# A planned attention and feed-forward kernel: another order of work, other assumptions about loads, and one third of a batch transposed by DMA

## The chip, the cores and the metric

The kernel runs on one core of one Trainium2 chip. The metric is device time in microseconds (us) of one execution. Engines: TensorE (PE for its matmuls, PEld for its weight loads), VectorE (DVE), ScalarE (ACT), GpSimd (POOL) and SyncE (SP). In this kernel POOL issues the loads and SP the stores and the DMA transposes; ScalarE issues two stores at the very end. Each engine executes its instructions in the order in which the program lists them.

## What is computed

An attention with squared relu, and a gated feed-forward block on its result:

```python
scores = np.matmul(q, k.transpose(0, 1, 3, 2)) / np.sqrt(64)
attn_out = np.matmul(np.maximum(scores, 0.0) ** 2 / 448, v)     # q, k, v: (8, 12, 448, 64) float32
x = attn_out.transpose(0, 2, 1, 3).reshape(8 * 448, 768)
out = (gelu(x @ w_gate) * (x @ w_val)) @ w_out                   # 768 x 1536 twice, 1536 x 768
```

The output is 3584 x 768 in float32.

## The kernel before

The inputs are loaded by casting DMAs to bf16. A batch of 448 tokens and 12 heads is handled in thirds of four heads, written (b, m). For a third, q and k are loaded (two DMAs), transposed to qkT, multiplied to scores (`add_scores`, L692), passed through relu on ScalarE (L729) and squared on VectorE (L738), and multiplied with v (`add_values`, L768), which gives x transposed. All products use 64 x 64 quarters of the array and go through the helper on L397. Work called lo uses one row half of the array and work called hi the other, and the two halves run beside each other.

A third is transposed in one of two ways. `add_transposes` (L644) does it on TensorE, in two groups of 14 transposes (L662), with a copy on VectorE after each (L666). `add_dma_transposes` (L490) regroups q and k with one copy on VectorE (L499), and SP then issues two DMA transposes (L504). Batches 0 and 1 go through TensorE, later ones by DMA, except for the thirds listed in `ON_PE` (L350). A DMA transpose waits until the load issued last before it has landed, and a load waits for the DMA transposes issued before it ("pace").

The feed-forward part of batches 0 and 1 is computed plainly (`add_gate_value`, L1002), that of the batches from 2 on partly in pairs with seven products instead of eight (`add_pair`, L893), with sums of weights (ws) and of x (ts) made on VectorE. The second matrix (`add_product`, L1149) is done in 14 groups gr of 256 tokens, in seven products named 1 to 7 (chain 1 7 2 6 4 5 3), also from sums (wt, s). Each product's bank is read into osb, by a copy on ScalarE or VectorE (L1217) or an addition on VectorE (L1215). When both halves of a row tile are done, SP stores it with two DMAs, one for each half of 64 rows (L1233). The first tile of the last group is stored by column halves, one part by SP and one by ScalarE.

The weights w_gate and w_val come in six chunks (`load_w12`, L433: wg, then wv), called w0 to w5 here, and w_out in four (`load_wo`, L442). The order of all loads after those of batch 0 is written out in `LOADS` (L30): w is the next chunk of both weights, q the next third's q and k, v the next third's v, o the next chunk of w_out. POOL issues them in that order. qk16 has room for two thirds: a load of q and k has to wait until the transposes of the third two before it have read theirs. v has room for three. At most eight loads are in flight.

The order of TensorE's units after the start is planned before anything runs. `LINE` (L12) is a list of units in order of preference. `run_plan` (L104) plays the whole program through with a cost for each operation, takes among the first 60 units of the list the one that can start earliest, and puts ScalarE's, VectorE's and SP's operations in the order in which they become ready. What it assumes of loads: the bytes over a rate (`arrivals`), one after the other, 2.0 us to landing, and a margin (`LATE`, 1.0) for loads after batch 0. The order found in this way is fixed in the program; the plan's times are not.

## Time and profile before

| | |
|---|---|
| median of 3 runs | 405.67 us (404.91 to 411.33) |
| the profiled execution | 406.31 us |
| its span, first to last instruction | 404.5 us |
| granted clock of TensorE, mean | 0.998 |
| products on L397, from the first to the last | 6.5 to 399.2 us |
| transposes of q and k on TensorE (L662) | 15 groups, 7.4 to 63.8 us |
| DMA transposes | 32, 74.6 to 291.3 us |

How to read the rows below. In the slices each digit is the busy share of a fortieth of the span, in tenths. A row of waits gives the engine, the operation and line that waited, what it waited for, then us in total, times, and the longest. A row of a stretch gives its bounds, its length, and for each engine the busy time with the number of instructions in brackets (with a line as filter, PE and PEld of that line alone), then granted clock, DMA share and GB/s. A row of the chain of waits gives start, duration and what ran. A row of the timeline gives start, duration, engine, line and operation, out<-in, and in square brackets the idle time before it and what ended it. A row of groups gives busy time, the mean in ns, and the idle time before with its releasers. PEq, SPq and ACTq are sequencers, which issue DMAs.

### The profile page before, as it was taken

What the parts mean: (1) busy time and instruction counts of PE and PEld (TensorE: products, weight loads), DVE (VectorE), ACT (ScalarE), POOL (GpSimd) and SP (SyncE); (2) the same over time, 40 slices, a digit from 0 to 9 for tenths busy, and PEclk for the clock granted to TensorE, in tenths of its full rate; (3) what the DMA queues carried; (4) which work ended last, traced back from release to release, by engine and by line L of the source; (5) the groups of instructions that cost most, each with busy time, mean ns of one, the idle gap of its engine ahead of it and who ended that gap; (6) DMA issues with size and microseconds to landing.
All of it is one profiled execution on the core that took longest, in us unless ns stands there. A gap on an engine that the chain in (4) does not pass through costs nothing.

```text
span 404.5 us, 18664 instructions
## 1 busy us (share of the span) xinstructions
PE 394.6 (98%) x8533; PEld 347.7 (86%) x8536; DVE 299.4 (74%) x514; ACT 244.9 (61%) x367; POOL 74.0 (18%) x120
## 2 busy tenths in 40 slices
PE   7999999999999999999999999999999999999994
PEld 3456887998999978889999899999999999889993
DVE  2886885977778858889867698787977865777562
ACT  4856684675676676657876667584776643553120
POOL 7547432140122201310312103110110000000000
PEclk9999999999999999999999999999999999999999
DMA  7999999597569787824777988744551321000245
GB/s 104 156 176 196 198 196 138 103 174 127 96 90 181 132 149 119 121 53 73 95 142 95 235 137 137 109 64 71 45 98 42 81 55 29 2 3 3 62 120 138
DMA packets 71567, 43.94 MB, mean 109 GB/s; under 512 B 32448, under 2 KB 68032, under 8 KB 71488
## 3 DMA queue, kind: packets, MB, share of 16 engines
q0 software_dynamic: 37152, 24.39, 44.3%
q1 hardware_dynamic: 34176, 18.16, 22.0%
q8 instruction: 67, 1.10, 1.1%
q10 hardware_dynamic: 160, 0.20, 0.1%
q14 instruction: 12, 0.10, 0.1%
HBM read 48.76 MB, written 11.01 MB: 148 GB/s over the span
## 4 chain that ended last, share of the span: by engine, by line
PE 88%; DMA 7%; DVE 1%; issue 1%; POOL 1%; ACT 0%; SPq 0%; DVEq 0%; POOLq 0%
PE ff L397 77%; PE sp L397 7%; DMA qk<-in_k_dram 4%; DMA wv<-in_moe_w_val_dram 2%; PE sp L662 1%; PE ff L1395 1%; DMA qkT<-qkr 1%; PE ff L583 1%; POOL qk L457 1%; PE ff L662 0%; DVE qkr L499 0%; DVE osb L1217 0%; DVE uT L1028 0%; DVE attnT L738 0%; PE ff L625 0%
## 5 line engine op out<-in xcount | busy, mean ns | idle before, releaser
L397 PE MATMUL ff<-xT,wg 64*64 64x448 bf16 x1872 | 189.2, 350 | 0.5 <-DVE uT L1028 0.5
L729 ACT ACTIVATE attnT<-sp 128x896 bf16<-128x896 f32 x168 | 152.0, 919 | 48.5 <-PE sp L397 47.3
L397 PE MATMUL ff<-xT,wv 64*64 64x448 bf16 x1440 | 153.5, 350 | 0.5 <-DMA wv<-in_moe_w_val_dram 0.4
L397 PEld LDWEIGHTS <-wv 64*64 64x64 bf16 x1872 | 111.3, 107 | 11.7 <-DMA wv<-in_moe_w_val_dram 0.8
L397 PEld LDWEIGHTS <-wg 64*64 64x64 bf16 x1872 | 110.6, 107 | 10.4 <-issue 0.8
L738 DVE TENSOR_TENSOR attnT<-attnT 128x1792 bf16<-128x1792 bf16 (+1 forms) x98 | 92.3, 953 | 15.5 <-ACT attnT L729 15.1
L397 PE MATMUL ff<-attnT,v 64*64 64x448 bf16 (+1 forms) x768 | 83.8, 327 | 0.1
L397 PEld LDWEIGHTS <-s 64*64 64x64 bf16 x1344 | 80.9, 107 | 2.0
L397 PE MATMUL sp<-qkT 64*64 64x448 bf16 (+1 forms) x768 | 77.2, 333 | 0.8 <-ACT qkT L633 0.6
L397 PE MATMUL ff<-wo,s 64*64 64x384 bf16 x672 | 61.6, 323 | 0.0
L397 PEld LDWEIGHTS <-uT 64*64 64x64 bf16 x912 | 54.4, 107 | 1.4 <-issue 0.7
L397 PE MATMUL ff<-wt,s 64*64 64x384 bf16 x672 | 53.9, 323 | 0.0
L397 PE MATMUL ff<-ts,ws 64*64 64x448 bf16 x432 | 52.8, 349 | 0.0
L397 PE MATMUL ff<-ts,wv 64*64 64x448 bf16 x432 | 51.8, 349 | 0.4 <-DVE ts L876 0.4
L472 POOL DMA_DIRECT2D v<-in_v_dram x48 | 29.7, 628 | 119.3 <-ACT attnT L729 54.7
L397 PEld LDWEIGHTS <-v 64*64 64x64 bf16 x768 | 46.9, 107 | 4.1 <-issue 0.4
L397 PE MATMUL ff<-wo,uT 64*64 64x384 bf16 x576 | 48.1, 323 | 0.4 <-issue 0.4
L1028 DVE TENSOR_TENSOR uT<-gel,ff 128x448 bf16<-128x448 bf16 x60 | 37.0, 618 | 14.1 <-PE ff L397 12.4
L1023 ACT ACTIVATE gel<-ff 128x448 bf16<-128x448 f32 x60 | 32.5, 542 | 21.2 <-PE ff L397 20.0
L397 PEld LDWEIGHTS <-qkT 64*64 64x64 bf16 x768 | 37.9, 107 | 7.3 <-issue 3.9
L397 PEld LDWEIGHTS <-ws 64*64 64x64 bf16 x648 | 40.6, 106 | 3.4
L945 DVE TENSOR_TENSOR part<-ff,part 128x448 f32<-128x448 f32 x54 | 32.8, 621 | 9.3 <-PE ff L397 6.6
(60 smaller groups left out, 382.4 us busy)
## 6 DMA issues: line engine op xcount, KB each, us to landing
out_dram<-osb SPq DMA_DIRECT2D x54, 192.0 KB, 3.2
v<-in_v_dram POOLq DMA_DIRECT2D x48, 128.0 KB, 5.3
qk<-in_q_dram POOLq DMA_DIRECT2D x23, 224.0 KB, 5.2
qk<-in_k_dram POOLq DMA_DIRECT2D x23, 224.0 KB, 5.7
wg<-in_moe_w_gate_dram POOLq DMA_DIRECT2D x6, 384.0 KB, 9.4
wv<-in_moe_w_val_dram POOLq DMA_DIRECT2D x6, 384.0 KB, 10.1
wo<-in_moe_w_out_dram POOLq DMA_DIRECT2D x4, 576.0 KB, 9.5
qkT<-qkr SPq DMA_TRANSPOSE x32, 3.3
```

Source lines behind the costliest of these rows:

```text
L397: return nc.tensor.matmul(o, lhsT, rhs, start=start, stop=stop, skip_group_check=onto, tile_position=(P * row, P * col))
L457: op = load(4 * (h1 - h0) * S * D, lambda: nc.gpsimd.dma_start(tile_of(), src[b, h0:h1].rearrange("h (p c) d -> p h (c d)", c=SC)), deps, ...
L472: return nc.gpsimd.dma_start(v16[b, m][HALF[i], :, :, :], v[b, h0:h1].rearrange("h (p c) d -> p h c d", c=SC)[:, :, c0:c0 + VC, :])
L583: nc.tensor.matmul(t[:, :], warm[:, 0:128], warm[:, :], start=True, stop=True)
L662: nc.tensor.transpose(t[HALF[j], c, :], src[:, 2 * r + j, c, :], ident[:, :], tile_position=(0, P * j))
L729: relu.ins = nc.scalar.activation(duo["a"][:, u % 2, :, :], box[0][:, :, 0:S], AF.Relu).ins
L738: nc.vector.tensor_tensor(a[:, part], a[:, part], a[:, part], op=ALU.mult)
L945: rd.ins = nc.vector.tensor_tensor(t[:, :], box[0][:, 0:S], t[:, :], op=ALU.add).ins
L1023: nc.scalar.activation(gel[b, fc][:, :], box[0][:, 0:S], AF.Gelu)
L1028: u_op[b, fc].ins = nc.vector.tensor_tensor(uT[b][:, fc, :], gel.pop((b, fc))[:, :], box[0][:, 0:S], op=ALU.mult).ins
L1395: nc.tensor.matmul(t[HALF[j], :], warm[:, HALF[j]], warm[:, :], start=True, stop=True, tile_position=(0, P * j))
```

## The change

- The constants that the plan assumes change: a load counts as ready 0.3 us later, a wait for a free slot or for a transpose costs 0.5 us more (`WAKE`), arrivals after batch 0 take 6% longer (`SLOW`), and the margin is 3.0 us instead of 1.0 (`LATER_BY`) except for w0 to w4 and q and v up to third (2,0). The plan now also counts stores as DMA time (`stored`).
- `LOADS` has another order: w0, q and k of (1,0) and (1,1), w1, q and k of (1,2) and (2,0), v of (1,0) and (1,1), w2, w3, w4, v of (1,2) and (2,0), w5, and so on. Before it was q and k of (1,0), w0, q and k of (1,1), v of (1,0), w1, q and k of (1,2), w2, w3, q and k of (2,0), v of (1,1) and (1,2), w4, q and k of (2,1), w5.
- `LINE` has another order of units.
- w_out is loaded in eight DMAs, one for each chunk and column half; products on a half wait for that half.
- `ON_PE` keeps (2,0) alone: (2,1) is transposed by DMA.
- The last read of the last group is split between ScalarE and VectorE, and in the last two groups the second half of each store is issued by ScalarE.

```diff
--- before.py
+++ after.py
@@ -10,25 +10,25 @@
 
 
 LINE = """
-2 o s c2 2D1 s 0 s 0 2E6 o 4F1 0 0 0 s o d5 s 1 1 a1 1 s 5 0 1 b1 o a6 1 0 s a7 f6 0 2D2 1 2C2 0 s
...
+s 1 d4 s 1 s 2C1 s 1 0 2F5 0 0 6A4 s 1 4C2 2D3 2B1 h6 c7 o 1 o 0 0 2F2 a5 o 3 s s s s c6 o a3 2 0
...
 """

 LOADS = """
-q w q v w q w w q v v w q w v v q o o v o q o q v q q v q v q v v q v q v v q q v q v q v q v q v
+w q q w q q v v w w w v v w q q v o v q o q o o q v v q v q q v v q v q v q q v v q v q v q v q v
 q v v
 """
 
@@ -46,6 +46,7 @@
         self.gates = []
         self.start = self.end = None
         self.queued = 0.0
+        self.stored = 0.0
         self.place = 0
         self.open = False
 
@@ -60,7 +61,7 @@
         if len(self.ends) < self.size or key is not None and key in self.keys:
             return 0.0
         op = self.ends[-self.size]()
-        return None if op is None or op.end is None else op.end + self.lag
+        return None if op is None or op.end is None else op.end + (op.lag if self.lag is None else self.lag)
 
     def take(self, last, key=None):
         if key is None or key not in self.keys:
@@ -98,6 +99,7 @@
 BANK = 0.3
 SPARE = 1
 FLIGHT = 8
+WAKE = 0.5
 ALONE = True
 
 
@@ -148,9 +150,10 @@
     def ready(op):
         t = known.get(op)
         if t is not None and op in arrivals:
+            t += 0.3
             if len(landed) >= FLIGHT:
-                t = max(t, landed[-FLIGHT])
-            t = max(t, alone)
+                t = max(t, landed[-FLIGHT] + WAKE)
+            t = max(t, alone + WAKE)
             if any(x.queued and known[x] <= t for x in able["SP"]):
                 return None
         if t is not None and op.queued and landed:
@@ -285,6 +288,10 @@
             dma = max(dma, op.end) + arrivals[op]
             op.lag = dma + 2.0 + op.margin - op.end
             landed.append(dma + 2.0)
+        elif op.stored:
+            dma = max(dma, op.end) + op.stored
+            op.lag = max(5.0, dma + 2.7 - op.end)
+            last = max(last, dma + 2.0)
         elif op.queued:
             dma = max(dma, op.end) + op.queued
             op.lag = dma + 2.0 - op.end
@@ -347,8 +354,10 @@
     FB = 4
     FILL = 30.0
     EARLY = 2
-    ON_PE = ((2, 0), (2, 1))
+    ON_PE = ((2, 0),)
     LATE = 1.0
+    LATER_BY = 3.0
+    SLOW = 1.06
 
     NP = 3
     RING_V, RING_T, RING_H, RING_L, RING_A, RING_O, RING_E = 3, 3, 2, 2, 4, 4, 5
@@ -441,8 +450,10 @@
 
     def load_wo(i):
         rows = slice(i * WOG * 128, (i + 1) * WOG * 128)
-        wo_op[i] = load(4 * WOG * 128 * d_model, lambda: nc.gpsimd.dma_start(
-            wo[i][:, :, :], moe_w_out[rows, :].rearrange("(c p) f -> p c f", p=128)), rate=410e3)
+        for g in range(NG):
+            cols = slice(g * OGS, (g + 1) * OGS)
+            wo_op[i, g] = load(4 * WOG * 128 * OGS, lambda cols=cols: nc.gpsimd.dma_start(
+                wo[i][:, :, cols], moe_w_out[rows, cols].rearrange("(c p) f -> p c f", p=128)), rate=400e3)
 
     def load_qk(b, i, h0, h1, deps=()):
 
@@ -832,7 +843,7 @@
     stages_last = {"X": "3", "Y": "4", "Z": "2"}
     opens = "1", "7", "2"
     uT, gel, gel_op, u_op = {}, {}, {}, {}
-    osb_ring = Ring(RING_O, 5.0)
+    osb_ring = Ring(RING_O, None)
     gel_ring, part_ring, reads_u, reads_x = Ring(RING_G), Ring(RING_M), {}, {}
     GS, RS = 0.189, 0.1625
     G, R = KC * GS, FC // 2 * RS
@@ -1060,7 +1071,7 @@
                                   wo[i + 2][:, :, left], wo[i + 2][:, :, right])
             for n in (3, 2, 4):
                 wt[n, i] = wpool.tile([128, WOG, OGS], bf16, name=f"wt{n}{i}", tag=f"wt{n}{i}")
-            have = [wo_op[i], wo_op[i + 2]]
+            have = [wo_op[x, g] for x in (i, i + 2) for g in range(NG)]
             for n, out_, x, y, op in ((3, wt[3, i][:, :, :], b22, b12, ALU.subtract),
                                       (2, wt[2, i][:, :, :], wt[3, i][:, :, :], b11, ALU.add),
                                       (4, wt[4, i][:, :, :], b21, wt[2, i][:, :, :], ALU.subtract),
@@ -1083,7 +1094,7 @@
     def weight_ready(name, fc):
 
         i = fc // WOG
-        return {"1": lambda: wo_op[i], "2": lambda: wo_op[i + 2], "3": lambda: wo_op[i + 2],
+        return {"1": lambda: wo_op[i, 0], "2": lambda: wo_op[i + 2, 0], "3": lambda: wo_op[i + 2, 1],
                 "4": lambda: wt_op[4, i], "5": lambda: wt_op[1, i], "6": lambda: wt_op[2, i],
                 "7": lambda: wt_op[3, i]}[name]()
 
@@ -1207,10 +1218,13 @@
                           "6": (t1, left, False), "4": (t1, left, True),
                           "7": (t1, right, False), "5": (t1, right, True)}[name]
 
-        def emit_read(copy=nc.scalar.copy):
+        def osb_of(t):
             if t not in osb:
                 osb[t] = opool.tile([TT, d_model], f32, name="osb", tag="osb")
-            o = osb[t][:, cols]
+            return osb[t]
+
+        def emit_read(copy=nc.scalar.copy):
+            o = osb_of(t)[:, cols]
             if added:
                 ins = nc.vector.tensor_tensor(o, box[0][:, 0:OGS], o, op=ALU.add)
             else:
@@ -1224,6 +1238,19 @@
                 other=None if added else ("DVE", 0.52, lambda: emit_read(nc.vector.tensor_copy)))
         if not added:
             rd.takes = osb_ring, lambda: stored[t][-1] if t in stored else None, t
+        reads = [rd]
+        if final and name == "3":
+            def emit_half(copy, h):
+                part = slice(OGS + h * OGS // 2, OGS + (h + 1) * OGS // 2)
+                ins = copy(osb_of(t)[:, part], box[0][:, h * OGS // 2:(h + 1) * OGS // 2])
+                return ins
+
+            def emit_first():
+                rd.ins = emit_half(nc.scalar.copy, 0).ins
+
+            rd.other, rd.cost, rd.emit = None, 0.29, emit_first
+            reads.append(Op("DVE", 0.32, lambda: emit_half(nc.vector.tensor_copy, 1), [ops[1][-1]], lag=0.2, prio=0))
+            DVE.append(reads[1])
         (DVE if added else ACT).append(rd)
         st["read", name] = rd
         st["read", stage] = rd
@@ -1233,14 +1260,21 @@
             engine.dma_start(rows[c, :, part], osb[t][HALF[j], part])
 
         if name in "2345":
-            st["done", t] = [*st.get(("done", t), ()), rd]
+            st["done", t] = [*st.get(("done", t), ()), *reads]
             if final and t == t0:
-                SP.append(Op("SP", 0.6, lambda: emit_store(0, nc.sync, cols), [rd], prio=-1))
-                ACT.append(Op("ACT", 0.1, lambda: emit_store(1, nc.scalar, cols), [rd], prio=-1))
+                SP.append(Op("SP", 0.6, lambda: emit_store(0, nc.sync, cols), reads, prio=-1))
+                ACT.append(Op("ACT", 0.5, lambda: emit_store(1, nc.scalar, cols), reads, prio=-1))
+                SP[-1].stored = ACT[-1].stored = 0.25
             elif len(st["done", t]) == 2:
-                stored[t] = [Op("SP", 0.6, lambda j=j: emit_store(j), st["done", t], lag=2.5, prio=-1)
-                             for j in range(2)]
-                SP.extend(stored[t])
+                queues = (SP, "SP", 0.6, nc.sync), (ACT, "ACT", 0.5, nc.scalar)
+                stored[t] = []
+                for j in range(2):
+                    pool, name_, cost, engine = queues[j if gr >= FINAL - 1 else 0]
+                    op = Op(name_, cost, lambda j=j, engine=engine: emit_store(j, engine), st["done", t],
+                            lag=2.5, prio=-1)
+                    op.stored = 0.5
+                    stored[t].append(op)
+                    pool.append(op)
         for b in {b for tile in (chunks[1:] if "hold" in st else chunks) for b, _ in tile}:
             reads_u.setdefault(b, []).append(ops[1][-1])
         then(at, RS, *ops, box if name in opens else None, lambda: st["read", stages_last[stage]], ("p", gr, name))
@@ -1278,6 +1312,12 @@
         for op in POOL[n:]:
             op.token = x, at
     assert not any(todo.values())
+    for op in POOL:
+        if not hasattr(op, "token"):
+            continue
+        arrivals[op] *= SLOW
+        kind, at = op.token
+        op.margin = LATE if kind == "w" and at < 5 or kind in "qv" and at <= (2, 0) else LATER_BY
     add_weight_sums()
     for b, m in late:
         if (b, m) not in ON_PE:
```

More of the change, by code (lines that the diff above doesn't have):

```diff
@@ new lines @@
+3 c3 s 0 s 0 s s 0 0 s 2 1 s s s b6 e5 s 0 4D4 1 s s 1 o 4A5 s o 2D4 6B6 1 s o 2E4 3 1 0 s b3 2B2
+0 1 5 s 1 2 0 s 2A6 s 2A2 a4 o s b2 0 2E5 s 0 0 a7 s f6 1 s 2F1 n5 s 1 2C2 a2 1 2A1 4C3 2 s s 1 1
+g6 s 3 1 k4 o s 3 o c1 s 4A1 s 2A5 b1 s o 2F3 b7 o s s c5 s 2B7 c2 o s 4 f1 s s o s s b4 2E1 2 c4
+2C6 2A7 6 s 2A4 d7 o d6 2C4 s 5 s s 2 h4 s 4C7 2B5 4E1 s 2 s o e4 s s 2D2 2D6 s s o 4 6F5 6A2 3
+2C7 o s s s m5 2B4 4D6 m1 2 6A1 5 4A3 2B3 s s 4A6 2E2 s 6 2F6 o 3 f5 4 2C3 4A4 s s g1 2F4 s e3 o 4
+l6 4C5 3 s 2E6 2 s 2E7 s 2F7 o s s s 4 o 3 2E3 s j1 s s s e2 d3 e6 h3 s s e1 3 4C1 4F5 g5 e7 o s
@@ L28 @@
+m2 6E2 6D2 n1 6 7 6 m7 7 7 7 l3 n7 k2 7 7 m4
 """
 LOADS = """
-q w q v w q w w q v v w q w v v q o o v o q o q v q q v q v q v v q v q v v q q v q v q v q v q v
+w q q w q q v v w w w v v w q q v o v q o q o o q v v q v q q v v q v q v q q v v q v q v q v q v
 q v v
```

21 lines of the change are left out of this document (7 added, 14 removed).

## The prediction

> **What bounds the kernel now.** I read the page's busy shares and its 40 slices first, then the waits of TensorE, then busy time by stretches, then the chain of waits where a stretch falls short.
>
> ```profile
> PE 394.6 (98%) x8533; PEld 347.7 (86%) x8536; DVE 299.4 (74%) x514; ACT 244.9 (61%) x367; POOL 74.0 (18%) x120
> PE   7999999999999999999999999999999999999994
> ...
> DMA  7999999597569787824777988744551321000245
> ```
>
> TensorE is busy all the way; DMA is full only over the first 70 us or so. TensorE's own waits are short:
>
> ```profile
> PE ff L397 <- DVE uT L1028: 0.5, 1, 0.5
> ...
> PE ff L397 <- DMA wv<-in_moe_w_val_dram: 0.4, 1, 0.4
> ...
> PE ff L397 <- DVE ts L876: 0.4, 1, 0.4
> ```
>
> Busy time alone hides how much a stretch computes, because matmuls of two row halves overlap. So I also count matmuls of line 397, which does all products:
>
> ```profile
> 28.00:30.00 2.00, 1.17 (x14) 0.49 (x10) 1.00 1.42 196
> 30.00:32.00 2.00, 1.56 (x20) 0.61 (x16) 1.00 1.46 197
> 32.00:34.00 2.00, 1.56 (x28) 0.68 (x30) 1.00 1.37 203
> 34.00:40.00 6.00, 6.00 (x130) 3.81 (x130) 1.00 1.38 195
> 52.00:60.00 8.00, 8.00 (x182) 7.28 (x174) 1.00 1.39 196
> 60.00:64.00 4.00, 1.86 (x25) 0.56 (x22) 1.00 0.86 106
> ```
>
> From 34 us on the rate is 130/6 = 21.7 a us, then 182/8 = 22.8. It falls short at the start, where the third batch is transposed on TensorE (60 to 64), at two waits shown below, and in the tail. All else is products that no part of the change removes, so the gain is bounded by these places.
>
> **The change part by part.** The sum is made against the profiled execution: 406.31 us, of which the span is 404.5. It lies 0.64 above the median of the runs, 405.67.
>
> **One third of batch 2 leaves TensorE.** Before, thirds (2,0) and (2,1) take two groups of 14 transposes each. At 22.8 a us, the 25 matmuls of 60 to 64 are worth 1.10 us, so four groups cost 2.90 us, 0.72 each. Two go: 1.45. The lower bound is the time of the groups themselves in the chain, 0.51 each, 1.02 for two:
>
> ```profile
> 61.45 0.51 PE sp L662 x14
> ```
>
> The third then goes the way of the sixteen others, a regrouping copy on VectorE and two DMA transposes from SP:
>
> ```profile
> L499 DVE COPY qkr<-qk 128x1792 bf16<-128x1792 bf16 x16 | 9.9, 621 | 4.5 <-DMA qk<-in_k_dram 4.0 <-issue 0.5
> ...
> L666 DVE COPY qkT<-sp 128x896 bf16<-128x896 bf16 x10 | 5.8, 619 | 4.3 <-PE sp L662 4.3
> ```
>
> ```profile
> qkT<-qkr SPq DMA_TRANSPOSE x32, 3.3
> ```
>
> VectorE does one copy of 0.62 instead of two (line 666), so it gains. SP issues two transposes more, before its first store. A pair of transposes waits until the loads issued before have landed, and later loads wait for it: two landings of 3.3 us, 6.6 us at most, in which no load runs. That is hidden as long as products of batches 0 and 1 are left; uncovered it would cost up to those 6.6 us.
>
> By the Trainium skill, Perfetto Trace Analysis, Identifying the Most-Contended Engine, matmul busy share misjudges the distance from the limit and weight-load busy share judges it. Here the trace agrees at 60 to 64: by matmul busy time alone (nearly no idle) two groups are worth 1.02, by the counts 1.45, and the weight-load row falls with the counts. What that rule would give elsewhere is a rival below.
>
> **Weights ahead of the second batch.** In the load list w0 moves ahead of the first q and k of batch 1; w2, w3 and w4 move behind q and k of (1,2) and (2,0) and v of (1,0) and (1,1).
>
> ```profile
> 9.85 2.48 POOL L472 DMA_DIRECT2D v<-in_v_dram  x4
> 15.81 0.62 POOL L457 DMA_DIRECT2D qk<-in_q_dram  x1 [3.49 <-PE ff L662]
> ...
> 17.02 0.86 POOL L437 DMA_DIRECT2D wg<-in_moe_w_gate_dram  x1
> ...
> 30.21 0.64 POOL L457 DMA_DIRECT2D qk<-in_q_dram  x1 [4.92 <-PE sp L662]
> ```
>
> The queue is in order. w0 sits behind a q load that waits 3.49 us for transposes to free its buffer. Moved ahead, it issues right behind the four v loads of batch 0, at 12.3 instead of 17.0. The chain shows what hangs on it:
>
> ```profile
> 17.85 9.90 DMA wv<-in_moe_w_val_dram
> ...
> 27.79 1.21 PE ff L397 x12
> ```
>
> ```profile
> 17.18 9.05 ACT L729 ACTIVATE attnT<-sp 128x896 bf16<-128x896 f32 x11 [0.39 <-PE sp L397]
> ```
>
> TensorE waits 0.4 us for wv (row above). With that gone, the end of batch 0's attention is next: ScalarE runs its activations without a gap up to 26.2, the squares, the last values and their read follow, and no load is in that path. So I take 0.4. The first counts bound the rest: from 28 to 34 there are 62 matmuls, at 21.7 a us 2.86 us, and the two thirds of batch 1 transposed there are four groups at 0.72, 2.88; of 6 us only 0.26 is unexplained. At best the part gains 0.4 + 0.26 and a little where transposes pack closer, about 1.0; at worst nothing.
>
> Against it stands that w2 now waits for more. q of (2,0) needs the buffer that the transposes of (1,1) free, about 32 us. An estimate at 196 GB/s of bf16 (rows from 28 to 40), from 18.5 when batch 0's last v is there: w0, two thirds of q and k and w1, 768 + 2 x 448 + 768 KB, by 31.2; two more thirds and two of v, 2 x 448 + 2 x 256 KB, by 38.6; w2's 768 KB by 42.6. Until then, from 28.5, TensorE has w0's rest (4.0 us; a pair of weight loads feeds 96 matmuls, 96/21.7 = 4.4) and w1's 4.4, four thirds of transposes (8 x 0.72 = 5.8) and some 5 us of scores and values: 19.2 us of work for 14.1. So nothing is charged; the cover is 5.1 us.
>
> **Output weights in eight loads.** The bytes stay. POOL, busy 18%, issues four more at 0.76: 3.0 us.
>
> ```profile
> L397 PE MATMUL ff<-wo,uT x576: 319/323/347, 100.1 to 388.8; 64*64 64x384 bf16 x192
> ...
> L444 POOL DMA_DIRECT2D wo<-in_moe_w_out_dram x4: 750/755/777, 63.5 to 82.6; - x4
> ...
> DMA to landing us min/median/max: 8.2/9.5/11.8
> ```
>
> The last of them lands by 82.6 + 11.8 = 94.4 and the first product starts at 100.1, so 5.7 us cover a later arrival, and beyond that products of batch 1 do. Zero; beyond the cover each us late costs a us at most.
>
> **Loads counted as longer and later.** This adds no instruction; it changes which copy or matmul stands behind which on the in-order engines. Two waits are of this kind:
>
> ```profile
> 139.88 7.39 DMA qk<-in_k_dram
> ...
> 147.35 0.63 DVE qkr L499
> ...
> 166.90 7.09 DMA qk<-in_k_dram
> ...
> 174.07 0.63 DVE qkr L499
> ```
>
> A k load takes over 7 us; the regrouping copy is already at the head of VectorE's queue, so the sums and gate products behind it, which do not need the load, wait too, and TensorE after them. VectorE loses 4.0 us so (its row for line 499, above). TensorE loses less: the waits for ts and uT are 0.4 + 0.5 of idle time, and since a matmul shows 0.35 where four start every 0.18 (4/21.7), each wait hides 0.17 more: 1.24. A margin of 3 us instead of 1 puts about 2 us more of other work ahead of each copy, where 4.0 us in two places is 2.0 each. I take 1.0. The bounds are 1.24 gained and, since a new order can stand on a new wait as long as the largest of these, about 0.6 lost.
>
> **The tail.** After the last matmul at 399.16 come a read and the stores:
>
> ```profile
> 395.68 5.51 SPq L1233 DMA_DIRECT2D out_dram<-osb  x7
> ...
> 399.16 0.56 DVE L1217 COPY osb<-ff 128x384 f32<-128x384 f32 x1 [1.55 <-PE ff L397]
> 399.75 0.51 ACTq L1233 DMA_DIRECT2D out_dram<-osb  x1
> ```
>
> SP's seven stores are back to back and its last starts at 400.5 (next row), ScalarE's at 399.75: SP's queue alone is late by 0.75.
>
> ```profile
> L1233 SPq DMA_DIRECT2D out_dram<-osb x10: 466/588/944, 386.0 to 400.5; - x10
> ```
>
> With one half of each of the last groups' stores on ScalarE, the last issue follows the last read at once: 0.7 gained. The read is halved between ScalarE and VectorE. A copy of 448 columns beside the one of 384 at 399.16 gives the slope:
>
> ```profile
> L941 DVE COPY part<-ff 128x448 f32<-128x448 f32 x20 | 12.4, 622 | 4.6 <-PE ff L397 4.2
> ```
>
> 0.06 us for 64 columns, so 192 columns fewer take about 0.37 instead of 0.56: 0.2 gained. Together 0.9; at best 1.2, at worst 0.5 lost, one issue that stands on ScalarE ahead of a read.
>
> **The sum:** 1.45 + 0.4 + 1.0 + 0.9 = 3.75 less, so 406.31 - 3.75 = 402.6 against the profiled run and 405.67 - 3.75 = 401.9 against the median, which I give. The ends are 1.45 + 1.0 + 1.24 + 1.2 = 4.9 less (400.8) and 1.02 less with 0.6 + 0.5 back (405.75).
>
> **The rivals.** *The waits only move.* The order is new everywhere, and a plan corrected for two waits can have as many others. Then transposes and tail alone gain, 1.45 + 0.9: 403.3. For it speaks that the two waits are 1.2 us out of 400, hard to plan for.
>
> *The load stream runs late and TensorE starves* between 40 and 60 us, the mechanism on the other side. w2 stands behind two loads that wait for TensorE's transposes, as the 4.92 us of POOL at 30.21 shows. It decides from 8.9 us of lateness, the cover of 5.1 and the gain of 3.75: each us beyond 5.1 costs one. Late by two such waits, 9.8 us, it takes back 4.7 and the time is 406.6; over 2% slower needs w2 some 17 us late, four such waits. Against it speaks that DMA is kept full by the earlier w0.
>
> *More room than I count.* By weight-load busy share, 140 to 180 falls short:
>
> ```profile
> 120.00:140.00 20.00, 20.00 (x487) 19.19 (x482) 16.87 (x32) 12.98 (x18) 3.18 (x6) 1.00 0.89 146
> 140.00:160.00 20.00, 19.64 (x432) 16.01 (x425) 14.20 (x22) 13.01 (x20) 3.58 (x6) 1.00 0.82 145
> 160.00:180.00 20.00, 19.50 (x420) 16.08 (x416) 16.58 (x29) 11.98 (x21) 3.07 (x5) 1.00 0.60 96
> ```
>
> At 19.19 per 20 us, 40 us would hold 38.4; they hold 32.1, so 6.3 us would be free, 5.1 beyond the 1.24 counted: 401.9 - 5.1 = 396.8. That is what the Trainium skill's rule named above would make of it. Against it: within these 40 us the chain has a stretch of 76 matmuls in 3.50 us (46 ns each) and the best stretch late in the kernel 218 in 10.28 (47 ns), so the array is full there and what differs is how weight loads overlap.
>
> ```profile
> 155.10 3.50 PE ff L397 x76
> ...
> 275.12 10.28 PE ff L397 x218
> ```
>
> **How the numbers follow.** The forecast and its bounds have 0.64, the moved waits 0.18, the starved array 0.13 (0.05 of it over 2%), the larger gain 0.05. Two per cent, about what a measurement of this kernel can tell from no change, is 8.1 us: faster means below 397.6, slower above 413.8. Faster gets 0.04, slower 0.05, and the rest, 0.91, lies within. The likeliest alone spans 400.8 to 405.8. The range of 399.2 to 406.5 adds half of the larger gain and of the starved case.
>
> **What would show it.** Two transpose groups instead of four after 40 us, and no stretch of 4 us with only 25 products: the first term. wg issued near 12.3 and no wait on wv near 27: the second. VectorE's wait for k ahead of the regrouping copies below 1 us in sum: the third; if such waits stand elsewhere, the first rival. SP's last store within 0.2 us of ScalarE's, and both near the last read: the fourth. If TensorE has idle time or low counts between 38 and 60 us while POOL waits for transposes, the starved case holds, and the forecast is wrong by that time.

## The result, and the profile after

| | before | after |
|---|---|---|
| median | 405.67 us (404.91 to 411.33, 5 runs) | 402.60 us (401.73 to 403.88, 5 runs) |
| ratio, 95% interval | | 0.9919 (0.9892 to 0.9945) |
| profiled execution; its span | 406.31; 404.5 us | 403.23; 401.5 us |

The changed kernel is 0.8% faster, within the 2% called no change. The forecast was 401.9 us, 0.7 low. Between the profiled executions 3.1 us went, where the sum had 3.75. The ratios leave out executions over 1.5% above a kernel's fastest; only the kernel before and two experiments on it (e2, e3) had any, and the profiles of e2 and e3 are of such.

The page of the changed kernel begins like the old one:

```profile
PE 392.2 (98%) x8507; PEld 338.2 (84%) x8510; DVE 302.0 (75%) x519; ACT 243.6 (61%) x362; POOL 76.9 (19%) x124
```

The 26 TensorE instructions fewer are the two transpose groups (28), but for two that the traces miss. Of TensorE's waits, those for uT, ts and wv are gone; others are new:

```profile
PE sp L406 <- DMA qkT<-qkr: 0.6, 1, 0.6
...
PE ff L673 <- DMA qk<-in_k_dram: 0.4, 1, 0.4
PE sp L406 <- ACT attnT L740: 0.4, 1, 0.4
```

Busy time shows little, so I count the products as the prediction did: matmuls of line 397 before, line 406 after, by stretches. First the kernel before:

```profile
0.00:46.00 46.00, 29.69 (x482) 1.00 1.18 163
46.00:64.00 18.00, 15.86 (x328) 1.00 1.29 176
64.00:120.00 56.00, 55.97 (x1235) 1.00 0.79 124
120.00:140.00 20.00, 20.00 (x487) 1.00 0.89 146
140.00:180.00 40.00, 39.14 (x844) 1.00 0.71 120
180.00:260.00 80.00, 79.63 (x1826) 1.00 0.79 128
260.00:402.00 142.00, 139.12 (x3117) 1.00 0.29 57
```

and the kernel after:

```profile
0.00:46.00 46.00, 29.18 (x482) 1.00 1.18 161
46.00:64.00 18.00, 17.12 (x364) 1.00 1.37 191
64.00:120.00 56.00, 56.00 (x1250) 1.00 0.89 132
120.00:140.00 20.00, 19.37 (x465) 1.00 0.85 142
140.00:180.00 40.00, 40.00 (x874) 1.00 0.78 126
180.00:260.00 80.00, 79.79 (x1819) 1.00 0.76 123
260.00:402.00 142.00, 136.43 (x3068) 0.99 0.30 59
```

At 22.4 products a us (3117 in 139.12) the lead of the changed kernel, in products done by the same time, grows as follows: nothing by 46 us, +36 (1.6 us) where the third was transposed, +15 up to 120, -22 (1.0 us back) at 120 to 140, +30 (1.3 us) at 140 to 180, -7 up to 260. So two stretches gain about what the sum expected of them, the start brings nothing, and something new costs at 120 to 140.

The regrouping copies, which VectorE spent 4.5 us waiting in front of, wait no more; there are 17 now:

```profile
L510 DVE COPY qkr<-qk 128x1792 bf16<-128x1792 bf16 x17 | 10.5, 619 | 0.0
```

A third wait of this kind stands in the kernel before and not in the prediction, VectorE's longest single wait for a load: a sum of output weights stands at the head of its queue. It is gone too.

```profile
94.51 0.76 DVE L1068 TENSOR_TENSOR wt<-wo,wo 128x1152 bf16<-128x1152 bf16 x1 [2.78 <-DMA wo<-in_moe_w_out_dram]
```

The five kernels with the order of before (before, e1, e2, e3, e9) wait there 2.3 to 3.2 us and do 207 to 222 products from 90 to 100 us; the changed kernel, e6, e7, e8 and e11 do not wait and do 226 to 230 (e5, late by its double transposes, does not wait either and does 217). That is about 0.6 us between the means, and part of the +15 up to 120. e11 shows that the halved loads of w_out are not what removes the wait.

At the start wg of w0 is issued at 12.50 instead of 17.02, and the wait for wv is gone. But w2 is issued at 35.48 and 36.30 instead of 31.43 and 32.26, and its wv takes 8.6 us (the row below the three issues, a view of that one load), so it is there at 44.9; before it was at 41.4.

```profile
12.50 0.84 POOL L446 DMA_DIRECT2D wg<-in_moe_w_gate_dram  x1
...
35.48 0.90 POOL L446 DMA_DIRECT2D wg<-in_moe_w_gate_dram  x1
36.30 0.90 POOL L446 DMA_DIRECT2D wv<-in_moe_w_val_dram  x1
```

```profile
DMA to landing us min/median/max: 8.6/8.6/8.6
```

Around that landing TensorE runs short: 76 products from 42 to 46, where the kernel before has 96. The trace has no wait of TensorE for w2 itself; what is low is the number of products that the order has to put there.

```profile
42.00:46.00 4.00, 3.64 (x76) 1.00 1.46 197
```

The new cost at 120 to 140 stands in the chain of waits: scores wait for a DMA transpose that takes 4.52 us. SP issues its transposes only from 125.40 on; why so late is told under e11.

```profile
126.45 0.19 SPq L515
...
126.69 4.52 DMA qkT<-qkr
...
131.34 0.38 PE sp L406 x4
```

The tail, by a row each of the chain, of the timeline and of SP's queue:

```profile
396.47 0.37 DVE osb L1245
```

```profile
396.86 0.32 ACT L1245 COPY osb<-ff 128x192 f32<-128x192 f32 x1 [5.97 <-DVE osb L1245]
```

```profile
L1260 SPq DMA_DIRECT2D out_dram<-osb x53: 466/589/1645, 112.8 to 397.2; - x53
```

The halves of the last read do not run beside each other: ScalarE's waits for VectorE's, so the read takes 0.71 us (396.47 to 397.18) and not 0.37. SP's last store starts right behind it, as ScalarE's does, at 397.2. From the last matmul (its end, where the read can start) to the end of the span it was 404.5 - 399.1 = 5.4 us and is 401.5 - 396.4 = 5.1.

### The profile page after: what moved, and what is told of

Same layout as the page of the kernel before. It is cut to its first block, busy times and chain, and to the rows that moved or that the text cites. A ratio compares the mean times of both kernels' runs of the same rounds, so it can differ in the third digit from the quotient of the medians.

```text
span 401.5 us, 18623 instructions
## 1 busy us (share of the span) xinstructions
PE 392.2 (98%) x8507; PEld 338.2 (84%) x8510; DVE 302.0 (75%) x519; ACT 243.6 (61%) x362; POOL 76.9 (19%) x124
## 3 DMA queue, kind: packets, MB, share of 16 engines
q0 software_dynamic: 38752, 24.39, 44.9%
## 4 chain that ended last, share of the span: by engine, by line
PE 94%; DMA 3%; POOL 1%; issue 1%; ACT 0%; DVE 0%; SPq 0%; POOLq 0%
PE ff L406 84%; PE sp L406 8%; DMA qk<-in_k_dram 2%; DMA qkT<-qkr 1%; PE sp L673 1%; POOL qk L468 1%; PE ff L594 1%; PE ff L673 1%; ACT attnT L740 0%; DVE osb L1245 0%; ACT osb L1245 0%; POOL ident masks.py:199 0%; POOL ident masks.py:197 0%; SPq L515 0%; ACT xT L822 0%
## 5 line engine op out<-in xcount | busy, mean ns | idle before, releaser
L406 PEld LDWEIGHTS <-wg 64*64 64x64 bf16 x1872 | 108.4, 106 | 10.8
L749 DVE TENSOR_TENSOR attnT<-attnT 128x1792 bf16<-128x1792 bf16 (+1 forms) x98 | 92.3, 952 | 11.0 <-ACT attnT L740 10.4
L406 PEld LDWEIGHTS <-s 64*64 64x64 bf16 x1344 | 74.2, 107 | 5.3 <-issue 0.5
L406 PE MATMUL sp<-qkT 64*64 64x448 bf16 (+1 forms) x768 | 75.5, 328 | 1.9 <-DMA qkT<-qkr 0.6
L406 PE MATMUL ff<-wo,s 64*64 64x384 bf16 x672 | 59.1, 323 | 0.0
L406 PEld LDWEIGHTS <-uT 64*64 64x64 bf16 x912 | 52.5, 107 | 3.1
L406 PE MATMUL ff<-ts,ws 64*64 64x448 bf16 x432 | 49.9, 349 | 0.0
L406 PE MATMUL ff<-ts,wv 64*64 64x448 bf16 x432 | 49.5, 349 | 0.0
L406 PE MATMUL ff<-wo,uT 64*64 64x384 bf16 x576 | 46.3, 323 | 0.0
L406 PEld LDWEIGHTS <-qkT 64*64 64x64 bf16 x768 | 36.3, 106 | 9.3 <-issue 4.9
```

Of the source, the lines that this page charges most:

```text
L406: return nc.tensor.matmul(o, lhsT, rhs, start=start, stop=stop, skip_group_check=onto, tile_position=(P * row, P * col))
L749: nc.vector.tensor_tensor(a[:, part], a[:, part], a[:, part], op=ALU.mult)
```

## The experiments

Each changes one thing and leaves the order of all other instructions as it was, but for e8, which also has the whole read of e7, for one copy at the end of e1 that goes from ScalarE to VectorE, and for e4, e10 and e12, where the plan makes another order. The medians stand beside the kernel before on the same chip. Counts of products from the same view, for kernels with the order of before and of after:

| us | before | e1 | e3 | e9 | after | e5 | e7 | e11 |
|---|---|---|---|---|---|---|---|---|
| 0 to 46 | 482 | 512 | 484 | 509 | 482 | 468 | 490 | 499 |
| 46 to 64 | 328 | 337 | 332 | 332 | 364 | (325) | 367 | 367 |
| 120 to 140 | 487 | 486 | 488 | 485 | 465 | 489 | 487 | 451 |
| 140 to 180 | 844 | 839 | (766) | (870) | 874 | 871 | 865 | 876 |

In brackets where the experiment's own edit acts. The start varies by 30 products between executions with the same instructions; 46 to 64 and 140 to 180 vary by about 10, outside the long executions that e3 shows.

**e5: the price of two transpose groups.** The 28 transposes of (2,0) are done twice, into the same place.

```diff
-            for c in range(SC):
+            for c in [*range(SC)] * (2 if (b, m) == (2, 0) else 1):
```

> The changed kernel with the 28 transposes of third (2,0) done twice, into the same place, so that TensorE does as many as with two thirds on it; all orders unchanged. Theory (a group costs what the products beside it lose, 0.72 us): 1.45 us slower than the changed kernel's profile, and in the stretch from 56 to 62 us two more groups. Rival (a group costs its own 0.51 or less, because the array drains once for both): 1.0 us or less.

404.57 us (402.41 to 406.75), ratio 0.9950 (0.9916 to 0.9984). The stretch that holds the groups, in after and then in e5:

```profile
56.00:64.00 8.00, 7.12 (x148) 1.00 1.27 184
```

```profile
56.00:64.00 8.00, 5.79 (x121) 1.00 1.19 167
```

27 products fewer are 1.2 us, 0.6 a group. That lies between the rival's 1.0 and the theory's 1.45, and a count that is good to a few products does not separate the two. (The other products missing from 46 to 64 lie ahead of the groups, where this execution is already late from the start.) The end moves by 1.3 us in the profiled spans and by 2.0 in the medians, with overlapping intervals.

**e2 and e6: the place of w0.** e2 is the kernel before with w0 ahead of q and k of (1,0); e6 the changed kernel with w0 behind them. The issues are moved in GpSimd's queue; in terms of the list of loads, e2 and then e6:

```diff
-q w q v w q
+w q q v w q
```

```diff
-w q q w q q
+q w q w q q
```

> The kernel before, with w0 issued ahead of q and k of (1,0), every other engine's order unchanged. Theory: wv0 is there long before 27.8, the transposes of (1,0) start about 1.1 us earlier, and as nothing later on TensorE waits for more, 0.4 to 1.1 us of it reaches the end. Rival (the lead is given back): ScalarE and the later loads hold the work between 30 and 60 us as before, and the end moves by less than 0.3 us.

> The changed kernel with w0 issued behind q and k of (1,0) again, as before; all other orders unchanged. Theory (the early w0 is worth what the prediction took, or more): wg0 issues near 17, TensorE waits for wv0 near 27.7, and the end is 0.4 to 1.1 us later. Rival (the lead at 28 us is given back at 43.9, where TensorE waits for ScalarE in any case): the wait at 43.9 shrinks by as much, and the end moves by less than 0.3 us.

e2: 406.28 us (404.50 to 412.39), ratio 1.0011 (0.9984 to 1.0039). e6: 403.46 us (401.78 to 405.07), ratio 0.9933 (0.9904 to 0.9963). Up to 46 us e2 has 510 products, between the 482 to 512 of the order before; e6 has 480, beside 468 to 499 of the changed order. In e6 wg of w0 goes out at 16.92 instead of 12.50 and TensorE has no wait for wv either. The transposes of (1,0) start at 27.55 to 28.93 us in the five profiles with w0 second (before, e1, e3, e9, e6) and at 26.96 to 28.88 in six with w0 first (the changed kernel, e2, e5, e7, e8, e11). If the place of w0 is worth the 0.4 us of the sum, it is lost in this spread: the runs neither show it nor exclude it.

**e8: ScalarE's wait at 45 us.** TensorE's 0.4 us there is a wait for an activation that stands behind a copy of x, which itself waits. e8 puts the copy behind the next activation, and reads the last bank whole.

```diff
+    if e == "ACT" and op in MOVED["xT"] and "done" not in MOVED:
+        MOVED["done"] = True
+        kept.append(op)
+        return []
+    if e == "ACT" and kept:
+        return [op, kept.pop()]
```

> The changed kernel with the whole last read, and with ScalarE's first copy of x (at 43.9 us) put behind the next activation of the scores, which had its data earlier. Theory (TensorE waits at 44.7 for that activation only because it stands behind the copy): the wait of 0.4 us and the low counts around it go, 0.8 us is gained, 1.0 with the read. Rival (other work is missing there: w2 lands at 44.9): the counts stay low until 46 us and less than 0.3 us is gained.

402.19 us (401.58 to 403.44, 7 runs), ratio 0.9912 (0.9881 to 0.9942). TensorE's wait is gone and 42 to 46 is busy throughout, but it holds no more products to speak of:

```profile
42.00:46.00 4.00, 4.00 (x80) 1.00 1.45 198
```

80 against 76, where the kernel before has 96. What is left to run before w2 is there keeps TensorE busy and fills less of it; the wait for ScalarE is not the cause of the low count. On the count the rival holds. The time does not decide: this is the fastest median of the study, 0.4 us below the changed kernel's and 0.9 below that of e7, which lacks only the swap, but the ranges overlap.

**e12: w2 one load earlier.** w2 ahead of the values of (1,1), with a list rearranged for it.

```diff
-w q q w q q v v w w w v v ...
+w q q w q q v w v w w v v ...
```

> The changed kernel with the third pair of gate and value weights issued one load earlier, ahead of the values (1,1) of the second batch instead of behind them, and a list rearranged for it by the plan's own time (397.75 us, against 395.6). Theory (the 1.2 us that the array starves at 43 to 46 us are the wait for the third pair of weights, which landed at 42.9 and 44.9): the pair lands about 1.3 us sooner, the low counts at 43 to 46 go for the most part, and the stretch 0 to 70 us gains 0.5 to 1.2 us; with the rest of the order as good as before, 401.4 to 402.1 us. Rival (the plan's own time decides, 2.2 us longer: what is gained at the start is given back where the rest had to move): 403.5 to 405.5 us.

404.81 us (403.89 to 407.12), ratio 0.9991 (0.9964 to 1.0018).

```profile
42.00:46.00 4.00, 4.00 (x96) 1.00 1.45 197
46.00:56.00 10.00, 10.00 (x208) 1.00 1.45 196
56.00:64.00 8.00, 7.12 (x139) 1.00 1.19 172
```

w2 lands 2.0 and 1.8 us earlier (at 40.9 and 43.1), and the count from 42 to 46 is 96 again, as the theory has it if the landing is what starves this stretch. But the 20 products are given back by 64 us (208 + 139 against 223 + 148 of the changed kernel, 24 fewer), and the theory's time falls; the rival's (403.5 to 405.5) holds. The list was rearranged together with the load, so this run does not separate what the landing did from what the list did, in the gain or in what was given back.

**e11: the output weights in four loads.**

```diff
-            wo_op[i, g] = load(4 * WOG * 128 * OGS, lambda cols=cols: nc.gpsimd.dma_start(
-                wo[i][:, :, cols], moe_w_out[rows, cols].rearrange("(c p) f -> p c f", p=128)), rate=400e3)
+            wo_op[i, g] = load(4 * WOG * 128 * OGS, None if g else lambda: nc.gpsimd.dma_start(
+                wo[i][:, :, :], moe_w_out[rows, :].rearrange("(c p) f -> p c f", p=128)), rate=400e3)
```

> The changed kernel with the output weights in four loads of 128 x 2304 elements again instead of eight of half the columns, each at the place of the first half; the order of all other instructions unchanged. Theory (the halves cost and bring nothing, as the sum had it): the time of the changed kernel within 0.5 us, 402.1 to 403.1, ratio 0.991 to 0.9935, and no wait of TensorE for an output weight in either. Rival 1 (two issues of about 0.8 us each per load hold up GpSimd's later loads): 0.5 to 1.5 us faster, the next loads behind each issued about 0.6 us sooner. Rival 2 (the first half has to be there earlier, the whole lands later): a wait of TensorE for wo of 0.3 us or more, and 0.5 to 2 us slower.

402.99 us (402.14 to 404.11), ratio 0.9941 (0.9920 to 0.9963); no wait of TensorE for wo. The halves are worth nothing that can be measured. Its profile has the largest cost at 120 to 140, by the same DMA transposes (PEld waits 1.6 us for one). Of the six profiled executions with the changed order, four have that cost, 451 to 469 products (e11, the changed kernel, e6, e8), and two have not, 487 and 489 (e7, e5): up to 36 products, 1.6 us.

```profile
120.00:140.00 20.00, 18.71 (x451) 1.00 0.77 122
```

The time of a transpose does not tell these executions apart: the four around 126 us land after 3.1 to 4.5 us in the changed kernel and after 4.0 to 4.7 in e7. The time of issue does. By the kernel's own pacing SP holds them until the last load of v is there. That load goes out at 117.05 and lands 8.2 us later in the changed kernel, at 116.04 and 4.9 us later in e7, and SP begins right behind it (the changed kernel, then e7):

```profile
125.40 5.64 SPq L515 DMA_TRANSPOSE qkT<-qkr  x4
```

```profile
121.15 7.55 SPq L515 DMA_TRANSPOSE qkT<-qkr  x4
```

In e6, e8 and e11 that load takes 8.9 to 10.4 us. In e5 SP begins later still, at 126.70, but there TensorE has the double transposes behind it and needs them later: it has done 2034 products up to 120 us, the changed kernel 2096.

**e3: the two waiting copies a little later.** Kernel before; copy (4,2) behind three more VectorE operations, (5,1) behind two, their DMA transposes after them.

```diff
+        behind = {(4, 2): 3, (5, 1): 2}
+        if (b, m) in behind:
+            MOVED.setdefault("copies", {})[copy] = behind[b, m]
+            MOVED.setdefault("after", {}).update({op: copy for op in tr_op[b, m]})
```

> The kernel before, with the two regrouping copies that VectorE waited for moved behind three and two more of VectorE's operations ((4,2) and (5,1)), all else in its order. Theory (the load's lateness costs only through the place of the copy): VectorE's wait for k goes from 4.0 us to under 1.5, the two TensorE waits for ts and uT go, and 1.24 us is gained. Rival (the waits only move): TensorE waits as long for the DMA transposes that now come later, and less than 0.4 us is gained.

409.8 us (404.16 to 414.61, 12 runs), ratio 1.0005 (0.9959 to 1.0051): neither theory. 5 of the runs lie at 404 to 405.4, 7 at 409.6 to 414.6. The profile is one of the latter, and shows a third wait, of the copy (5,0) that I had not moved:

```profile
172.65 0.63 DVE L521 COPY qkr<-qk 128x1792 bf16<-128x1792 bf16 x1 [5.14 <-issue]
```

The view names no releaser for it. Its k was issued late, behind a wait for the DMA transposes of (4,2), in the queue of GpSimd, and landed 3.6 us later, just before the copy:

```profile
169.00 0.62 POOL L479 DMA_DIRECT2D qk<-in_k_dram  x1 [11.87 <-DMA qkT<-qkr]
```

where the profiled execution of the kernel before issues it at 164.49. A load waits for transposes and a transpose for loads, so lateness of one goes on to the next, and at the end VectorE stands: TensorE waits 3.2 us for a partial sum. The loss does not end there. Matmuls of line 419 from 171 to 182 us:

```profile
171.00:172.00 1.00, 0.24 (x6) 1.00 1.23 190
...
174.00:176.00 2.00, 1.60 (x21) 0.62 1.19 187
176.00:178.00 2.00, 2.00 (x30) 0.53 0.32 50
178.00:182.00 4.00, 4.00 (x92) 1.00 0.61 119
```

The granted clock (the column behind the count) is 1.00 when TensorE comes to stand and falls behind the wait, to 0.62 and 0.53, until 178 us. A matmul takes 0.58 to 0.64 us there and 0.35 to 0.38 before and after. TensorE resumes at 174.4, and from there to 178 does 51 products where 3.6 us at the later rate (92 in 4) would hold 83: some 1.4 us lost beside the wait's 3.2, by this estimate. The lower clock follows the wait; it does not cause it. Of the 108 runs of the kernel before that stand beside the experiments, 15 are over 410 us, and 14 of these have a mean granted clock of 0.985 to 0.994; of the other 93, 85 have more.

The profiled execution of e2 (410.92 us), whose order here is exactly the kernel before's, has the same wait in the same place, and the clock behind it at 0.50 and 0.75:

```profile
172.40 0.63 DVE L517 COPY qkr<-qk 128x1792 bf16<-128x1792 bf16 x1 [4.85 <-issue]
```

**e9: the copies (5,0) and (5,1) five operations later,** so that this wait cannot arise.

```diff
+        behind = {(5, 0): 5, (5, 1): 5}
```

> The kernel before, with the regrouping copies of (5,0) and (5,1) each moved behind five more of VectorE's operations; their DMA transposes are issued 6 us and 11 us after them, so nothing on SP moves. Theory (a late k load costs only because the copy stands at the head of VectorE's queue): between 160 and 180 us VectorE waits for no k load any more, TensorE's wait for uT goes, 0.7 us is gained against the profile of before and more against its longer runs, whose highest times, over 410, go. Rival (the waits only move): the same loss stands a few us later, and the times spread as before.

405.18 us (403.49 to 407.93), ratio 0.9993 (0.9965 to 1.0022).

```profile
L521 DVE COPY qkr<-qk 128x1792 bf16<-128x1792 bf16 x16 | 9.9, 618 | 1.8 <-DMA qk<-in_k_dram 1.8
```

```profile
140.00:180.00 40.00, 40.00 (x870) 1.00 0.68 110
```

One wait of 1.8 us is left (copy (4,2)), the stretch has 870 products where the kernel before has 844 and the changed one 874: 1.2 us, as the prediction had it. None of 12 runs is above 408, while of the kernel before's own 18 beside it 4 are (408.51 to 415.75). The median gains 0.65 us and the ratio without the longest 0.3, both within the interval. That the longest went rests on little: e1, whose order here is that of the kernel before, has none above 408.09 in its 12 runs either.

**e4: the margin of 2.5 us instead of 3.0,** the list unchanged.

```diff
-    LATER_BY = 3.0
+    LATER_BY = 2.5
```

> The changed kernel with one assumption of the plan moved a little: the margin of late loads is 2.5 us instead of 3.0, the list of units left as it is. The plan's own time goes from 395.6 to 403.5. Theory (the list fits only the assumptions under which it was found, and the plan tells the sign): 5 to 8 us slower than the changed kernel, 408 to 411. Rival (the order hardly matters as TensorE is full anyway): within 1.5 us of the changed kernel, 401 to 404.

408.57 us (406.92 to 409.95), ratio 1.0059 (1.0030 to 1.0088), some 6 us slower than the changed kernel, as the theory had it. TensorE, VectorE and ScalarE wait for no load in 140 to 260 us; the products are fewer all along it:

```profile
140.00:180.00 40.00, 39.87 (x837) 1.00 0.69 124
180.00:260.00 80.00, 80.00 (x1781) 1.00 0.69 117
```

This list belongs to the one set of assumptions that it was made for; under another the order is merely worse.

**e10: the old assumptions with a list of their own,** so that the list is not the difference.

```diff
-    LATER_BY = 3.0
-    SLOW = 1.06
+    LATER_BY = 1.0
+    SLOW = 1.0
 LINE = """
...
```

> The changed kernel with the earlier assumptions on loads (a load as long as its bytes take, no factor of 1.06, and landing 1.0 us late instead of 3.0), and, since a list fits only the assumptions it was made for, with a list of its own: the changed kernel's list, rearranged by moving pieces for as long as the plan's own time fell. That time is 394.8 us, against 395.6 of the changed kernel, so by the plan alone the two are equal or this is 0.8 faster. Theory (the later landings are what keeps waits for loads out of the order): order and loads again trust a landing that comes 2 to 3 us later than planned; at least one copy or value step is placed ahead of its load, VectorE or TensorE waits for a load between 60 and 300 us where the changed kernel has none of over 0.5 us, and the span exceeds the plan by over 8 us: 403.5 to 407 us, ratio to the kernel before 0.995 to 1.005. Rival (any list that is good under its plan would do; the changed assumptions only came along): 401.5 to 403.5 us, ratio 0.990 to 0.9945, no such wait.

405.35 us (402.71 to 408.10, 12 runs), ratio 0.9985 (0.9948 to 1.0022). Its plan says 394.8 us, the changed kernel's 395.6, so by the plan it was the better one; the chip makes it 2.7 us slower. VectorE waits for loads again, 0.7 us for a k and more for output weights:

```profile
92.41 0.76 DVE L1079 TENSOR_TENSOR wt<-wo,wo 128x1152 bf16<-128x1152 bf16 x1 [6.19 <-DMA wo<-in_moe_w_out_dram]
```

A sum of output weights stands at the head of VectorE's queue 6.19 us before its load is there, the gate products behind it come late, and 64 to 120 has 74 products fewer than the changed kernel's 1250, 3.3 us:

```profile
64.00:120.00 56.00, 53.78 (x1176) 1.00 0.92 137
```

The theory holds and the rival falls, with the one list that was tried.

**e1: the tail's stores on two queues.** The kernel before, with the second half of each store of the last two groups on ScalarE's queue.

```diff
-                stored[t] = [Op("SP", 0.6, lambda j=j: emit_store(j), ...) for j in range(2)]
+                    pool, name_, cost, engine = queues[j if gr >= FINAL - 1 else 0]
+                    op = Op(name_, cost, lambda j=j, engine=engine: emit_store(j, engine), ...)
```

> The kernel before, with one thing of the change: the second half of each store of the last two groups is issued by ScalarE. The rest of the order stays, but for one copy at the end that goes from ScalarE to VectorE. Theory (the queue of SP is what is late): the last issue on SP moves from about 0.8 us behind the last read to directly behind it, and the span ends about 0.75 us earlier. Rival (the transfers share the same DMA engines, so only the issue moves): the landing takes as much longer, 0.3 us or less is gained.

406.9 us (403.77 to 408.09), ratio 1.0018 (0.9990 to 1.0046). Span 405.4; the last read, right behind the last matmul, and SP's last store:

```profile
400.23 0.56 DVE osb L1217
```

```profile
L1233 SPq DMA_DIRECT2D out_dram<-osb x53: 466/550/1460, 122.0 to 400.8; - x53
```

The last store is issued 0.6 us after the last matmul (400.8 - 400.2) instead of 1.4 (400.5 - 399.1), but the end comes 4.6 us after that issue instead of 4.0. Of 0.8 us, 0.2 is left, so the rival holds: the last stores, sent two at a time over two queues, land 3.0 and 3.2 us after their issue, where SP's last in the kernel before took 2.7. The Trainium skill says as much, DMA: Bandwidth & Descriptors, Rules for kernel authors: spreading DMAs over issuing engines saves issue time and no more, since they share the same DMA engines.

**e7: the last read whole,** by VectorE.

```diff
-        if final and name == "3":
+        if False:
```

> The changed kernel with the last read in one piece on VectorE instead of halves on ScalarE and VectorE; all else as it is. Theory (the halves run one behind the other, because ScalarE's half waits for VectorE's: 0.36 + 0.32 + gaps, 0.71 us): the read takes 0.56 us and the end comes 0.15 us earlier. Rival (as predicted, the halves save time): 0.2 us later. The trace of the last 6 us decides, the times cannot.

403.1 us (402.31 to 404.46), ratio 0.9931 (0.9902 to 0.9960).

```profile
396.33 0.56 DVE osb L1231
```

0.56 us instead of 0.71, and the end comes 401.3 - 396.3 = 5.0 us after the last matmul, as with the split (5.1). The split brings nothing.

## Why the prediction was right or wrong

**One third off TensorE, 1.45 us: right.** 46 to 64 has 36 products more, 1.6 us, and e5 prices two groups at 1.2 by the counts. The cover named for the transposes that SP issues instead held in all but one place: the transposes around 126 us cost up to 1.6 us in four of six executions (e11 most) and nothing in two (e7, e5). I had called landings of 3.3 us hidden as long as products are left; what counted is that scores of one unit wait for one pair, that SP issues the pair only when a load of v is there, and that this load took 8.2 us in the changed kernel and 4.9 in e7. Whether this pair would come late with (2,1) on TensorE too was not tried.

**Weights ahead of the second batch, 0.4 us: the step that failed.** Moving w0 gave nothing that can be told from the spread of the start (e2, e6). I read the 0.4 us wait for wv in one profile as a cost; the start varies by 30 products, 1.3 us, between executions. Worse, the step charged nothing for w2, with a cover of 5.1 us. w2 came 2.3 us later than my estimate (44.9 for 42.6), well within the cover, and still 42 to 46 has 20 products fewer, 0.9 us. The cover was a sum of work, and a sum does not say that the work can run as fast as before: from 43.2 to 44.0 us the changed kernel's trace has products with v alone, and no gate product beside them. All five profiles with w2 late and no other delay have 73 to 80 products there (the changed kernel, e6, e7, e8, e11), all five with the order of before 94 to 99. That it is the landing of w2 is likely, not shown alone: e12 brings it forward and has 96 again, but with another list. Between the profiled executions the part is 0 at 46 us (482 and 482), 20 ahead up to 42 (414 and 394) and 20 back behind it; by the means of the table's four executions of each order (497 and 485) it is -12 products, -0.5 us, less than the start's own spread.

**Output weights in eight loads, 0: right** within what e11 can tell.

**Loads counted longer and later, 1.0 us: right in mechanism, a little larger.** The two waits are gone from VectorE, 140 to 180 has 30 products more, 1.3 us (bound: 1.24), and e9 gets 1.2 in that stretch from moving two copies alone. e10 speaks for the assumptions and not only a better list: with the old ones, a list that is good under its own plan puts a sum 6.2 us ahead of its load. The same sum is the wait that I left out: I listed two, but the kernel before has a third, 2.78 us for output weights at 94.5 us, which is gone too; if it is what makes the difference at 90 to 100, it is worth about 0.6 us. No run changes it alone. What I had not seen either is that such waits make the long executions of the kernel before: its runs beside the experiments go up to 415.75, those with the changed order of e6, e7 and e11 stay within 401.78 to 405.07. That long executions have the wait of copy (5,0) is shown in two profiles, e2 and e3; that removing it removes them is not shown (e9, beside e1).

**The tail, 0.9 us: right in place, wrong in size, 0.3.** The 0.75 us of SP's queue was an issue time; the later end of the stores took most of it back (e1). The split read is serial and brings nothing (e7).

**The sum.** 1.6 + 0 + 1.3 + 0.3 = 3.2 us, beside 3.1 between the profiled executions. The other stretches nearly cancel: +15, -22 and -7 products up to 260 us are -0.6 us, and from 260 on the rate is 22.49 a us instead of 22.41, +0.5 us over 136.43, which no part of the sum had. That the forecast came within 0.7 us is therefore luck in part: two terms were too small and two too large, and what it had not named, the loss at 120 to 140 and the gains up to 120 and behind 260, nearly cancels. All these parts are read from one pair of executions.

**The rivals.** *The waits only move* (403.3) is as near in time as the forecast, but not in cause: a wait did come at 126 us, and not in every execution, while 140 to 180 kept its gain. *The array starves* holds in place (42 to 46 us, with w2 behind loads that wait for transposes) at 0.9 us, a fifth of its price. *More room than I count* falls: 140 to 180 is busy throughout with 874 products, 30 more and not the 138 that 6.3 us would be (6.3 x 21.9). The weight-load share, by which, beside the share of peak arithmetic, the Trainium skill (Perfetto Trace Analysis, Identifying the Most-Contended Engine) judges the room, fell from 86% to 84% while the kernel became faster; here it follows how work overlaps, and counts of products tell the room.

**Open.** Why the load of v ahead of the DMA transposes takes 8.0 us or more in five executions and 4.9 in e7 was not tried, nor why ScalarE's half of the last read waits for VectorE's. The counts leave out records that the trace misses, so a few products either way mean nothing.

## What to carry to other kernels

Where engines run in order, an operation that stands at the head of its queue before its load is there blocks all that needs no load; plan loads by what their landing takes in the trace, and read the spread of the runs as well as the median, since a chain of loads and transposes that wait for each other shows there first. A cover counted in microseconds of work is only as good as the work's own concurrency: look at what can still overlap without the late operand. When a transfer is late, look at what held its issue before you blame its duration. A queue that is late at the end is worth its issue time only if the transfers themselves do not land later for it.

## What the runs showed of the hardware that I had not expected

- With the last stores issued at once over two queues the span ends 4.6 us after the last issue, with SP's queue late it was 4.0: 0.8 us of issue time became 0.2.
- Executions of the same instructions differ by 30 products, 1.3 us, in the first 46 us, and executions of the same order by 36, 1.6 us, where a pair of DMA transposes is held by a load.
- Behind waits of TensorE of 2.9 us (e2) and 3.2 us (e3) its granted clock fell to 0.50 and 0.53 and was back at 1.00 by 178 us; in e3 that added some 1.4 us to the loss, by the estimate there.
